# Moving three weight and value requests in a lightning-attention plus feed-forward kernel

## Chip, cores and metric

The kernel runs on one core of one Trainium2 chip. The metric is the time of the device in microseconds (us); less is better. A core has TensorE (matrix products), VectorE, ScalarE and GpSimd (elementwise work), and SyncE (SP), which here only asks for transfers. Transfers (DMAs) are carried by 16 DMA engines that all queues share. In the profile the engines are named PE (its weight loads PEld), DVE, ACT, POOL and SP; a trailing q, as in SPq, is that engine's sequencer, which issues transfers.

## The reference

Two steps. First a block-wise linear attention with decay over 4 batches, 8 heads, 768 positions of 64 elements; then a two-layer feed-forward with the gate h * cos(h).

```python
for b in range(nb):                                   # blocks of 64 positions
    intra = np.einsum('bhic,bhjc->bhij', qb, kb) * Dmask[None]
    intra = np.einsum('bhij,bhjd->bhid', intra, vb)
    inter = np.einsum('bhid,bhde->bhie', qb * lam_pow[None], kv_state)
    out[:, :, sl] = intra + inter
    kv_state = lam_block * kv_state + np.einsum('bhsd,bhse->bhde', kb_dec, vb)
...
x = attn_out as (3072 tokens, 512)
h = x @ w_in            # w_in (512, 2048)
g = h * np.cos(h)
out = g @ w_out         # w_out (2048, 512), result in float32
```

## The kernel before

The 3072 tokens are 24 blocks of 128. The first four blocks are made in two "spans", each of two batches' neighbouring blocks, with a shorter start-up path; the rest come in pairs of blocks (the first pair after the spans, made by `prepare` for blocks 4 and 5, is what the change calls the third pair). The feed-forward runs over tiles of 4, 2, 2, 2, 2, 2, 2, 4 and 4 blocks: for each of 16 column blocks f of w_in, four matmuls make h (L705), ScalarE makes the cosine (L711), VectorE multiplies (L717); then w_out is applied, four f at a time (L749), and the result is copied out (L763) and stored.

For an attention block, q, k and v are loaded in float32. q and v are multiplied by powers of the decay (L341, L349), k is only cast (L345); then q and k are transposed on TensorE (L371), the scores are made (L419) and masked on VectorE (L424), the state is updated (L431, "ps_kv", which needs the scaled v and k), and the values are made (L480, L508). For the third pair ScalarE casts k, GpSimd and VectorE share q and v: the first block's v is scaled by GpSimd and the second block's by VectorE.

The weights are cast on their way in, by DMAs that GpSimd issues: w_in in six pieces (`W_IN = [2, 2, 2, 4, 4, 2]` column blocks of 128) and w_out in four, each piece with four of the 16 rows of blocks. q, k and v of the pairs are asked for by SP (256 KB each), those of the spans by SP (q, k) and by GpSimd (v). Order of the requests is in a string (L35), and `add_w`, `add_load` and `add_span_load` make the requests; their `deps` are transfers that must have landed before this one is issued, set in the loop at L788 to L799: where the kind changes between weights and activations, a request waits for an earlier one of the other kind.

```python
ORDER = "q0 k0 q1 k1 v0 v1 i0 i1 i2 i3 i4 i5 o0 o1 o2 q4 q5 k4 k5 o3"
```

`i2` is the third w_in piece, `o3` the last w_out piece; `v4` and `v5`, the third pair's v, follow from L783 to L785. So `q4` (SP, L266 in the trace) waits for `o1` to land, `o3` for `q4`, and `v4` for `k5`.

The order of instructions on each engine is made by a planner (`Planner.order`) from estimated durations, dependences and priorities, before the kernel is built; engines then run their own lists in order and wait for each other with semaphores. GpSimd's list at the start is: v of both spans, three w_in pieces, two scalings of the second span's k (`k_sp`, L564), three w_in pieces, three w_out pieces, a cast of the state (L679), the last w_out piece, then q and v of the third pair (L341, L349). SP's list after the spans' loads is q4, q5, k4, k5, v4, v5, then q, k and v of the next pair, then stores. The fourth w_in piece also waits for VectorE's first masking of the second span's scores (L588), by a dependence added by hand (L309).

Of the kernel before, what the change touches and what calls it, by code (L numbers as in the profile page):

```python
# [18 lines left out]
SPANS = 2  # L19
# [122 lines left out]
def kernel(  # L142
# [10 lines left out]
    nc = tc.nc  # L153
# [10 lines left out]
    first = [sum(TILES[:i]) for i in range(len(TILES) + 1)]  # L164
# [69 lines left out]
    w_in_sb = consts.tile([P, KD, D_FF], BF16)  # L234
    w_out_sb = consts.tile([P, KF, DM], BF16)
    w_in_src = moe_w_in.rearrange("(ko ki) f -> ki ko f", ki=P)
# [17 lines left out]
    load_t, issue_t = {}, {}  # L254
    last_issue = {}

    def dma(queue, us, issue_us, emit, prio, deps=(), get=None, ordered=True, lat=1.9):
        t = pl.add(queue, issue_us, list(deps) + [last_issue.get(queue) if ordered else None], emit, prio, get=get)
        if ordered:
            last_issue[queue] = t  # L260
        d = pl.add("DMA", us, [t], None, prio, lat=lat)
        d.issue = t
        return t, d

    def start(queue, o, x, deps):
        i = queue.dma_start(out=o, in_=x)  # L266
        for d in deps:
            tc.add_manual_dep(i.ins, d.issue.ins.ins.name, mybir.DependencyInfo(
                mybir.DependencyClass.Sync, mybir.DependencyReason.DATA), reason="order of loads")
        return i  # L270

    def add_span_load(name, src, x, prio, deps):
        def emit(_):
            if on_pool:
                t = span_v[x]
            else:
                if ("raw", x) not in live:
                    live["raw", x] = work.tile([P, 2, H, 2, D], F32, tag="g", name="sp_f")
                t = live[name, "sp", x] = live["raw", x][:, "qk".index(name[0])]
            return start(nc.gpsimd if on_pool else nc.sync, t.rearrange("u h s d -> u h (s d)"),  # L280
                         src[x, :, 0:2 * P, :].rearrange("h (u s) d -> u h (s d)", s=2), deps)

        on_pool = name == "v_f"
        issue, load_t[name, "sp", x] = dma("POOL" if on_pool else "SP", 1.5, 1.0 if on_pool else 0.5, emit, prio, deps,
                                           lat=0.95 if on_pool else 1.0)
        return load_t[name, "sp", x]

    def add_load(n, name, src, prio, deps=()):
        b, c = where(n)

        def emit(_):
            t = loads.tile([P, H, D], F32, tag=name, name=name)
            live[name, n] = t
            return start(nc.sync, t, src[b, :, c * P:(c + 1) * P, :].transpose([1, 0, 2]), deps)

        issue_t[name, n], load_t[name, n] = dma("SP", LOAD_US, 0.85, emit, prio, deps, get=name, lat=1.0)
        return load_t[name, n]

    w_t, w_late = {}, []

    def add_w(which, c, prio, deps=()):
        def emit(_):
            if which == "in":
                a, z = sum(W_IN[:c]) * P, sum(W_IN[:c + 1]) * P
                i = start(nc.gpsimd, w_in_sb[:, :, a:z], w_in_src[:, :, a:z], deps)
                if c == 3:

                    tc.add_manual_dep(i.ins, w_late[0].ins.ins.name, mybir.DependencyInfo(
                        mybir.DependencyClass.Sync, mybir.DependencyReason.DATA), reason="lines of instructions first")  # L309
                return i  # L310
            a, z = c * KF // WCH, (c + 1) * KF // WCH
            return start(nc.gpsimd, w_out_sb[:, a:z, :], w_out_src[:, a:z, :], deps)

        part = W_IN[c] / 4 if which == "in" else 1.0
        early = which == "in" and c < 3
        _, w_t[which, c] = dma("POOL", 2.68 * part, 0.8, emit, -2000.0 if early else prio, deps,
                               lat=1.2)
        return w_t[which, c]
# [231 lines left out]
    def add_span(x):  # L550
# [76 lines left out]
        so, kt, v_t = [[], []], [], [load_t["v_f", "sp", x]]  # L627
        for hp in range(2):
            eq, ek = QK[x]["q"][hp], QK[x]["k"][hp]
            a = pl.add(eq, us[eq], [load_t["q_f", "sp", x]], partial(prep, name="q", hp=hp, e=eq), pa(-0.9 + 0.1 * hp))  # L630
            kt.append(pl.add(ek, us[ek], [load_t["k_f", "sp", x]], partial(prep, name="k", hp=hp, e=ek), pa(-0.9 + 0.1 * hp)))
            if x:
                w_t["in", 3].issue.deps.append(kt[hp])
            outs = []
            for name, src in (("qT", a), ("kT", kt[hp])):
                e = OUTS[x][name][hp]
                t = pl.add("PE", MM(P, 4), [src, s_first if name == "kT" else None], partial(transposes, name=name, hp=hp), pa(-0.5 + 0.1 * hp), banks=1)
                outs.append(pl.add(e, 0.58 if e == "ACT" else 0.42, [t], partial(transposes_out, name=name, hp=hp, e=e), pa(-0.5 + 0.1 * hp)))
                t.bank_frees = [[outs[-1]]]
            s1 = pl.add("PE", 0.42, outs, partial(scores, hp=hp), pa(0.1 + 0.1 * hp), banks=2)  # L640
            if x and hp == 0:

                spans[0]["values"].deps.append(s1)
                s_first = s1
            so[hp] = [pl.add("DVE", 0.69, [s1], partial(scores_out, hp=hp, i=i), pa(0.1 + 0.1 * hp + 0.05 * i)) for i in range(2)]
            s1.bank_frees = [[t] for t in so[hp]]
            if x and hp == 0:
                w_late.append(so[hp][0])

        u = pl.add("PE", 0.42, v_t + kt + [spans[0].get("carried")], update, pv(0.1), banks=1)  # L650
        Uo_sp[x] = [pl.add(e, 0.4 if e == "ACT" else 0.42, [u], partial(update_out, h=h, e=e), pv(0.1))
# [12 lines left out]
    def add_span_state():  # L664


        def update(t):
            live["kv", 1] = bank(t.bank[0], [P, H, D], F32, "ps_kv")
            for h in range(H):
                for s in range(2):  # L670
                    for L, r in zip(spans, halves):
                        nc.tensor.matmul(live["kv", 1][r, h, :], lhsT=L["k"][:, s, h, :], rhs=L["v"][:, s, h, :],
                                         start=(h == 0 and s == 0), stop=True, skip_group_check=True)

        def state(_):
            nc.vector.tensor_copy(new_sum(1, 1), live["kv", 1])  # L676

        def state_16(_):
            nc.gpsimd.tensor_copy(new_S(1, 1), live["sum", 1, 1])  # L679

        u = pl.add("PE", 16 * QUART + SW, span_deps + [w_t["out", 0]], update, LATE, banks=1)
        x = pl.add("DVE", 0.69, [u], state, LATE)
        Uo[1, 1] = pl.add("POOL", 0.61, [x], state_16, LATE)
        u.bank_frees = [[x]]
# [103 lines left out]
    for at, name in enumerate(names):  # L788
        which, n = name[0], int(name[1:])
        soft = which in "io"  # L790
        deps = [kept[-3 if soft else -2]] if at and (names[at - 1][0] in "io") != soft else []
        if name == "o3":
            deps = [load_t["q_f", 2 * SPANS]]
        if soft:
            kept.append(add_w({"i": "in", "o": "out"}[which], n, at, [] if at < 9 else deps))
        elif n < SPANS and at < 9:
            kept.append(add_span_load(which + "_f", src[which], n, at - 2040, kept[0:1] if name == "v0" else []))
        else:
            kept.append(add_load(n, which + "_f", src[which], at, deps))  # L799

    idle = pl.add("SETUP", 0.0, [], None, -1e9, banks=1)
    for x in range(SPANS):
        add_span(x)
    w_t["in", 3].issue.deps += w_late
    add_span_state()
    for pr in range(SPANS, NBLK // 2):
        prepare(pr)
# [69 lines left out]
```

## Time and profile before

| what | value |
|---|---|
| runs | 8, from 205.78 to 207.75 us |
| median | 206.17 us |
| the profiled execution's own time | 205.97 us |
| its span, first to last instruction | 204.3 us |
| TensorE clock granted | 1.000 |
| TensorE busy | 195.3 us |
| VectorE, ScalarE, GpSimd busy | 113.4, 119.2, 64.7 us |
| HBM read, written | 27.27 MB, 6.29 MB |
| first matmul of the feed-forward (L705) | 15.35 us |
| first matmul with w_out (L749) | 30.61 us |
| landing of second and third w_out piece | 29.49, 32.0 us |

Times inside the span are counted from its start. A matmul's row is pipelined: its stated duration overlaps the next one's, so the distance between starts says more than the duration. In lists of waits a row gives the engine, the line that waited, what ended the wait, then total us, times and longest us. In the chain a row gives start, length and what was waited for or worked on.

### The profile page before, as it was taken

The page shows a single profiled execution, that of the slowest core. Times are in us where ns is not written, and L with a number is a line of the kernel's source. Part 1 is how long each engine was busy: PE and PEld are TensorE (multiplying, and loading weights), DVE is VectorE, ACT ScalarE, POOL GpSimd, SP SyncE. Part 2 cuts the span into 40 slices and gives each one's busy share as a digit, 9 for nine tenths or more (in the row PEclk, how much of TensorE's full clock was granted, in tenths as well). Part 3 has the DMA queues.
Part 4 walks back from the last instruction along what each step waited for, and adds up shares of the span by engine and source line. Part 5 has one row for each costly group of instructions (what it writes and reads, how often), then busy time and mean ns, then how long its engine had stood idle before and what let it go on. Part 6 is the DMA issues. An engine that isn't in the chain of part 4 may idle for free.

```text
span 204.3 us, 5936 instructions
## 1 busy us (share of the span) xinstructions
PE 195.3 (96%) x2457; PEld 117.5 (58%) x2485; DVE 113.4 (56%) x221; ACT 119.2 (58%) x232; POOL 64.7 (32%) x85
## 2 busy tenths in 40 slices
PE   6999999999999999999999999999999999999993
PEld 2467444547747848666658766755454444444463
DVE  2887783257953947559557574835687444444001
ACT  5978871128837868466649586745768555354120
POOL 5866004056036263616364244545400000000000
PEclk9999999999999999999999999999999999999999
DMA  4999999989889999999999899999900110111112
GB/s 123 319 190 196 203 202 219 198 196 226 211 205 219 251 219 235 219 196 252 185 262 145 201 226 197 248 153 266 213 0 6 51 51 0 51 55 51 51 71 83
DMA packets 96906, 33.94 MB, mean 166 GB/s; under 512 B 84336, under 2 KB 93936, under 8 KB 96880
## 3 DMA queue, kind: packets, MB, share of 16 engines
q1 hardware_dynamic: 89376, 28.78, 62.3%
q0 software_dynamic: 7360, 4.72, 16.4%
q8 instruction: 19, 0.31, 0.7%
q10 hardware_dynamic: 144, 0.07, 0.1%
q14 instruction: 7, 0.06, 0.1%
HBM read 27.27 MB, written 6.29 MB: 164 GB/s over the span
## 4 chain that ended last, share of the span: by engine, by line
PE 76%; DMA 14%; SPq 3%; POOL 2%; issue 2%; DVE 1%; ACT 0%; POOLq 0%; ACTq 0%
PE ps_f L749 35%; PE ps_h L705 34%; DMA w_out_sb<-in_moe_w_out_dram 6%; DMA v_f<-in_v_dram 3%; DMA sp_f<-in_k_dram 3%; SPq L266 3%; PE ps_o L480 2%; DMA k_f<-in_k_dram 2%; PE ps_kv L431 2%; PE ps_o L508 1%; PE ps_s L419 1%; POOL w_in_sb L266 1%; POOL k_sp L564 1%; DVE v_s L349 0%; POOL w_out_sb L266 0%
## 5 line engine op out<-in xcount | busy, mean ns | idle before, releaser
L717 DVE TENSOR_TENSOR g<-ps_h,cos 128x256 bf16<-128x256 f32 (+1 forms) x148 | 72.9, 503 | 51.4 <-ACT cos L711 50.4
L711 ACT ACTIVATE cos<-ps_h,halfpi 128x256 f32<-128x256 f32 (+1 forms) x148 | 75.8, 539 | 31.4 <-PE ps_h L705 31.0
L705 PE MATMUL ps_h<-xT,w_in_sb 128*128 128x256 bf16 (+1 forms) x587 | 91.3, 304 | 0.3 <-issue 0.2
L749 PE MATMUL ps_f<-w_out_sb,g 128*128 128x512 bf16 (+2 forms) x393 | 88.5, 362 | 2.2 <-issue 1.4
L705 PEld LDWEIGHTS <-w_in_sb 128*128 128x128 bf16 x592 | 57.1, 98 | 30.8 <-DVE xT L516 0.4
L749 PEld LDWEIGHTS <-g 128*128 128x128 bf16 x416 | 38.4, 98 | 35.7
L341 POOL TENSOR_TENSOR qk<-q_f,q_scale 128x512 bf16<-128x512 f32 x19 | 19.7, 1044 | 37.8 <-DMA q_f<-in_q_dram 27.0
L763 ACT COPY o_sb<-ps_f 128x512 f32<-128x512 f32 (+1 forms) x24 | 13.8, 574 | 30.0 <-PE ps_f L749 30.0
L349 POOL TENSOR_TENSOR v_s<-v_f,v_scale 128x512 bf16<-128x512 f32 x19 | 19.5, 1043 | 20.9 <-DMA v_f<-in_v_dram 17.2
L516 ACT CAST xT<-ps_o 128x512 bf16<-128x512 f32 x19 | 10.2, 588 | 11.3 <-PE ps_o L508 8.8
L424 DVE TENSOR_TENSOR s_m<-ps_s,mask 128x512 bf16<-128x512 f32 x20 | 12.9, 683 | 3.3 <-PE ps_s L419 3.0
L345 POOL CAST qk<-k_f 128x512 bf16<-128x512 f32 x18 | 11.0, 614 | 4.6 <-DMA k_f<-in_k_dram 4.5
L437 DVE TENSOR_TENSOR sum<-sum,ps_kv 128x512 f32<-128x512 f32 x15 | 10.2, 682 | 0.8
L442 ACT CAST S<-sum 128x512 bf16<-128x512 f32 x15 | 9.0, 615 | 0.8 <-DVE sum L437 0.7
L480 PEld LDWEIGHTS <-v_s 64*64 64x64 bf16 x320 | 4.3, 106 | 5.0 <-issue 4.4
L763 DVE COPY o_sb<-ps_f 128x256 f32<-128x256 f32 (+1 forms) x2 | 0.7, 358 | 11.2 <-PE ps_f L749 11.2
L480 PE MATMUL ps_o<-s_m,v_s 64*64 64x64 bf16 x320 | 6.4, 198 | 0.5
L837 PE MATMUL ps_idle<-blank 128*128 128x512 f32 (+2 forms) x8 | 5.4, 824 | 1.6 <-DVE blank L209 1.6
L588 DVE TENSOR_TENSOR s_m_sp<-ps_s,mask_sp 128x512 bf16<-128x512 f32 x8 | 5.1, 684 | 1.0 <-PE ps_s L583 1.0
L266 POOL DMA_DIRECT2D w_in_sb<-in_moe_w_in_dram x6 | 4.6, 777 | 1.7 <-DVE s_m_sp L588 1.7
L431 PE MATMUL ps_kv<-v_s,qk 64*64 64x64 bf16 x288 | 4.7, 194 | 0.2 <-DVE v_s L349 0.2
L679 POOL CAST S<-sum 128x512 bf16<-128x512 f32 x1 | 0.6, 607 | 13.0 <-DVE sum L676 13.0
(70 smaller groups left out, 79.3 us busy)
## 6 DMA issues: line engine op xcount, KB each, us to landing
q_f<-in_q_dram SPq DMA_DIRECT2D x20, 256.0 KB, 3.8
k_f<-in_k_dram SPq DMA_DIRECT2D x20, 256.0 KB, 4.6
v_f<-in_v_dram SPq DMA_DIRECT2D x20, 256.0 KB, 5.0
out_dram<-o_sb SPq DMA_DIRECT2D x19, 256.0 KB, 2.4
w_out_sb<-in_moe_w_out_dram POOLq DMA_DIRECT2D x4, 512.0 KB, 11.6
out_dram<-o_sb SPq DMA_DIRECT2D x9, 128.0 KB, 3.3
sp_f<-in_q_dram SPq DMA_DIRECT2D x2, 512.0 KB, 5.2
sp_f<-in_k_dram SPq DMA_DIRECT2D x2, 512.0 KB, 5.6
```

Of the source, the lines that this page charges most:

```text
L266: i = queue.dma_start(out=o, in_=x)
L341: vec[e].tensor_mul(new_qk()[:, 0, :, s], live.pop(("q_f", 2 * pr + s)), q_scale[:, c, :].unsqueeze(2).to_broadcast([P, H, D]))
L345: (nc.scalar.copy if early else nc.gpsimd.tensor_copy)(new_qk()[:, 1, :, s], live.pop(("k_f", 2 * pr + s)))
L349: vec[e].tensor_mul(live["v_s", 2 * pr + s], live.pop(("v_f", 2 * pr + s)), v_scale[:, c, :].unsqueeze(2).to_broadcast([P, H, D]))
L424: nc.vector.tensor_mul(t, live["s", pr][s], mask.unsqueeze(1).to_broadcast([P, H, D]))
L437: nc.vector.tensor_add(new, live["sum", pr, 0] if half else live["sum", pr - 1, 1], live["kv", pr][half])
L480: yield lambda h=h: nc.tensor.matmul(o[halves[h % 2], h // 2, m], lhsT=live["v_s", n0 + s][m, h, :], rhs=live["s_m", n0 + s][m, h, :], sta ...
L705: nc.tensor.matmul(t[:, :n], lhsT=w_in_sb[:, kd, f * P:(f + 1) * P], rhs=live["xT", i][:, kd, at], start=(kd == 0), stop=(kd == KD - 1))
L711: nc.scalar.activation(c[:, :n], live["h", i, f, at.start][:, :n], AF.Sin, bias=halfpi)
L717: nc.vector.tensor_mul(live["g", i][:, f, at], live.pop(("h", i, f, at.start))[:, :n], live.pop(("c", i, f, at.start))[:, :n])
L749: nc.tensor.matmul(live["f", i, j, piece][:, :width], lhsT=live["g", i][:, f, j * P:(j + 1) * P], rhs=w_out_sb[:, f, part], start=(f == 0) ...
L763: (nc.scalar.copy if eng == "ACT" else nc.vector.tensor_copy)(o[:, :width], live["f", i, j, piece][:, :width])
```

## The change

Three requests move. The third w_in piece (`i2`) now waits, in the planner, for the two scalings of the second span's k on GpSimd, so it stands behind them in GpSimd's list; before, the fourth piece had that condition, with one more on VectorE's masking, by plan and by semaphore, and this second one is dropped. The last w_out piece (`o3`) waits for the third to land in place of the third pair's first q. The third pair's first v (`v4`) waits for no landing of k any more. The instructions on all engines stay the same; GpSimd's list differs in the place of one request, and the other engines' lists don't differ.

```diff
-    w_t, w_late = {}, []
+    w_t = {}
 
     def add_w(which, c, prio, deps=()):
         def emit(_):
             if which == "in":
                 a, z = sum(W_IN[:c]) * P, sum(W_IN[:c + 1]) * P
-                i = start(nc.gpsimd, w_in_sb[:, :, a:z], w_in_src[:, :, a:z], deps)
-                if c == 3:
-
-                    tc.add_manual_dep(i.ins, w_late[0].ins.ins.name, mybir.DependencyInfo(
-                        mybir.DependencyClass.Sync, mybir.DependencyReason.DATA), reason="lines of instructions first")
-                return i
+                return start(nc.gpsimd, w_in_sb[:, :, a:z], w_in_src[:, :, a:z], deps)
...
             if x:
-                w_t["in", 3].issue.deps.append(kt[hp])
+                w_t["in", 2].issue.deps.append(kt[hp])
...
-            if x and hp == 0:
-                w_late.append(so[hp][0])
...
         if name == "o3":
-            deps = [load_t["q_f", 2 * SPANS]]
+            deps = [w_t["out", 2]]
+        if name == f"v{2 * SPANS}":
+            deps = []
...
-    w_t["in", 3].issue.deps += w_late
```

## The prediction

> **What bounds the kernel now.** I read the engine table first, then the waits of TensorE, then the chain of waits between 29 and 47 us, and last the order of time on single engines.
>
> ```profile
> PE 195.3 (96%) x2457; PEld 117.5 (58%) x2485; DVE 113.4 (56%) x221; ACT 119.2 (58%) x232; POOL 64.7 (32%) x85
> PE ps_idle L837 <- DVE blank L209: 1.6, 1, 1.6
> PE ps_f L749 <- issue: 1.4, 9, 0.2
> PE ps_t L572 <- POOL k_sp L564: 0.3, 1, 0.3
> PE ps_t L572 <- DVE k_sp L564: 0.3, 1, 0.3
> PE ps_kv L431 <- DVE v_s L349: 0.2, 1, 0.2
> ```
>
> The first row says that TensorE is busy 96% of the span; the others list its waits (engine, line, who ended it: total us, times, longest). Only two of them touch what is changed: 0.3 us for GpSimd's k_sp and 0.2 us for the scaled v. So the change can win little; what it can lose is a new wait.
>
> ```profile
> 16.97 12.52 DMA w_out_sb<-in_moe_w_out_dram
> 31.95 3.77 DMA k_f<-in_k_dram
> 35.73 0.37 SPq L266
> 36.15 6.68 DMA v_f<-in_v_dram
> 42.83 0.02 issue
> 42.85 0.81 DVE v_s L349
> 43.71 0.44 PE ps_kv L431 x30
> ```
>
> This is the chain (start, length, what). Second w_out piece lands at 29.49; the second k lands at 35.72, releases v's request, v lands at 42.83, and VectorE's scaling lets TensorE go on at 43.71. The chain reads as 14% DMA on the page, but TensorE works beside nearly all of it. What matters is where it stands still:
>
> ```profile
> 37.98 0.61 PE L371 MATMUL ps_t<-ident,qk 128*128 128x128 bf16 x8
> 43.31 0.22 PE L431 MATMUL ps_kv<-v_s,qk 64*64 64x64 bf16 x2
> 43.71 0.44 PE L431 MATMUL ps_kv<-v_s,qk 64*64 64x64 bf16 x30 [0.18 <-DVE v_s L349]
> ...
> 35.74 0.62 ACT L345 CAST qk<-k_f 128x512 bf16<-128x512 f32 x1 [0.32 <-DMA k_f<-in_k_dram]
> ...
> 31.48 0.61 POOL L679 CAST S<-sum 128x512 bf16<-128x512 f32 x1 [12.98 <-DVE sum L676]
> 33.46 0.75 POOL L266 DMA_DIRECT2D w_out_sb<-in_moe_w_out_dram  x1 [1.37 <-DMA q_f<-in_q_dram]
> 10.23 2.04 POOL L564 TENSOR_TENSOR k_sp<-sp_f,k_sp 128x512 bf16<-128x512 f32 x2 [0.23 <-DMA sp_f<-in_k_dram]
> 13.97 2.30 POOL L266 DMA_DIRECT2D w_in_sb<-in_moe_w_in_dram  x3 [1.70 <-DVE s_m_sp L588]
> ```
>
> The 32 matmuls of L431 take from 43.31 to 44.15, 0.84 us; the next group of the same kind takes 0.46 us at 56.85. So v's lateness costs 0.38 us in all. The reader should also keep the transposes of k at 37.98: they follow ScalarE's cast, which ends at 36.36.
>
> **What the Trainium skill says.** "DMA: Bandwidth & Descriptors", section "Queues, rings and completion order", says that an engine goes round the queues that have work, and drains one packet, of up to 64 descriptors, before it changes. The trace agrees as to holding out: v was asked for at 35.73, yet in the answer for 36.8 to 38.4 only GpSimd's queue q0 moves packets (the w_out piece asked for at 33.46). No place in it shows a young piece overtaking an older load. The same page, section "Anatomy of one DMA — SWDGE (gpsimd) path", gives a fixed 2.0 us; here the lone w_out piece took 6.4 from issue to landing. "Runtime: NRT & Kernel Launch", section "Instruction fetch mechanics", says that instructions come by DMA in 16 KiB blocks; the page agrees in size (q8: 19 packets, 0.31 MB).
>
> **The change part by part.** The profiled execution took 205.97 us (span 204.3, 1.67 around it); sums are made against it. The median of the runs, 206.17, lies 0.20 above. No instruction is added or removed on any engine: TensorE, VectorE, ScalarE and SP keep their order, GpSimd moves one instruction, and waits change.
>
> *Third w_in piece.* GpSimd's third issue (0.78 us, 9.21 to 9.99) goes behind its two scalings of k. They then have GpSimd from 9.21, but need k, which lands at 10.06 (4.07 + 5.99 in the chain), so they start at some 10.15 instead of 10.23, and end near 12.2 (VectorE's k_sp starts 0.09 after its landing of 6.99). Bounds: gain 0 to 0.1; I take 0.05, off the 0.33 wait of TensorE at 11.33.
> The piece itself is issued at about 12.25 instead of 9.21. Before, it needed 8.9 us to land (18.1). Its first user is the fifth column block, after 20 more matmuls of 0.109 from 16.91: 19.09. In the queue ahead stand v and two pieces, and the engines are full (0.85 MB of q0 alone in the answer for 10.0 to 14.5), so a later request mostly waits less: the next piece, of double size, took 6.2, and 12.25 + 6.2 = 18.5. Cost 0, hidden by the 28 matmuls of the first two pieces; if landing took 8.9 again, 12.25 + 8.9 - 19.09 = 2.1 us.
>
> *The fourth w_in piece without its wait for VectorE.* The 1.70 us idle of GpSimd before 13.97 goes. Pieces four to six and three of w_out follow at 12.25 + 0.77 = 13.0 instead of 13.97, all moved up by 0.95 in the one queue. They land one after the other at the engines' rate (29.49 and 32.0 for the last two: 2.5 us each), so landings move by 0 to 0.3; TensorE waits for none of them now. Gain 0. The removed wait is labelled as keeping lines of instructions ahead of the piece. Without it a block of TensorE's instructions may queue behind one piece more (2.5 us); TensorE's rows show no wait of that kind, so I take 0.
>
> *The third pair's v.* SP asks for it after k's issue ends (31.95 + 0.82 = 32.8), not at 35.73: 2.9 us sooner. SP's next requests (two q, two k, two v of the fourth pair, from 36.78) move up with it, and one of those took 4.13 to issue; nothing of TensorE waits for them. The scaling on VectorE can start when its two masks are done, 40.81 + 1.29 = 42.10, and must start by 43.31 - 0.80 = 42.5. So v has to come only 0.4 us sooner than 42.83 for the whole 0.38 to go. Bounds: gain 0 to 0.38; I take 0.38.
>
> *The last w_out piece.* It now waits for the third piece (17.70 + 14.3 = 32.0) instead of a q that landed at 32.9, and stands behind the cast that ends at 32.09. Between wait and issue lay 0.54 before, so it starts at 32.15 to 32.55, about 1.1 us sooner. Behind it on GpSimd stands the scaling of q (34.22), which then starts with q's landing at 33.8, 0.3 sooner; TensorE's transposes of q at 35.80 were not waiting. First use of the piece is at 42.36 and it landed at 39.86: no gain. Its traffic now meets the second k's. That is the rival below; I take 0.
>
> Sum: -0.05 - 0 - 0.38 - 0 = -0.43 us, that is 205.5 for the execution and about 205.75 for a median; rounded, 205.8. Late next is nothing: TensorE's other waits are 0.1 to 0.16 us each, at its own changes of shape.
>
> **The rivals.**
> A, the forecast: 205.8.
> B, slower: the last w_out piece overtakes k. Before, it was issued at 33.46, and narrow windows of the DMA answer show q0's first packets at 34.9, 1.44 later; now that is 33.6 to 34.0. The two k landed at 34.78 and 35.72, so the second was moving from about 34.0. If the piece comes first on even one engine, that k is later by one piece, 2.55, up to 3.55 with the near empty microsecond that the answer for 35 to 36 shows at its start. Slack: 37.98 - 0.62 - 0.05 - 35.72 = 1.57. Loss 1.0 to 2.0, net of 0.43: 0.55 to 1.55, middle 207.2. It decides from a k landing after 37.3. For it: v stood behind this piece before. Against it: k is asked for at 31.95, 0.2 to 0.6 us earlier, by the faster path.
> C, nothing: the piece goes before v as now, and one late engine keeps v's landing at 42.8; the wait for v stays. 206.1. Against it: the idle microsecond at 35 to 36 is filled, which is more than 0.4.
> D, the third w_in piece lands after 19.1, or instructions come late: +0.5 to +2.1, 207.3.
> E, a gain that I don't see, from other loads coming sooner: 205.0. Against it: TensorE's remaining waits don't hang on loads.
>
> **How the numbers follow.** A 0.53, B 0.25, C 0.13, D 0.05, E 0.04. A measurement can tell about 0.5%, 1.03 us, from no change. Slower by that: half of B, all but a little of D, 0.03 for what I overlook: 0.20. Faster: E and the far edge of A: 0.05. Same: 0.75. The range goes from A less 0.5 (both waits of 0.33 and 0.38 gone, and noise) to the upper part of B: 205.3 to 207.3.
>
> **What would show it.** Right: k_sp starts at 10.1 to 10.2; the third w_in issue stands at 12.25 and lands before 19; v is issued near 32.8 and the group of L431 runs its 32 matmuls in 0.46; the cast of the second k stays near 35.7. B shows as an idle TensorE before the transposes at 37.98 with ScalarE's cast named; D as a wait of L705 near 19 us. I am wrong if a wait of over 0.2 appears on TensorE that is not among these.

## The result and the profile after

The changed kernel takes 208.63 us in the median (11 runs, 207.36 to 212.48) against 206.30 (32 runs of the kernel before beside it, 205.60 to 207.75): a ratio of 1.0106 [1.0081, 1.0131], slower. All ratios here leave out runs over 1.5% above the fastest of the same kernel as disturbed, among them three of the changed kernel (210.92, 211.19, 212.48), though these turn out below to be part of the effect.

The profiled execution took 210.14 us, with a span of 208.4; before, 205.97 and 204.3. So 4.1 us are to be found. All line numbers of the changed kernel are lower: L366 is L371 of before (transposes), L340 is L345 (cast of k), L426 is L431 (state), L742 is L749 (w_out), L414 is L419 (scores).

From the page of the kernel after, the engine table and the granted TensorE clock in 40 slices of 5.2 us:

```profile
PE 197.1 (95%) x2457; PEld 118.3 (57%) x2485; DVE 113.6 (54%) x221; ACT 119.3 (57%) x232; POOL 64.8 (31%) x85
...
PEclk9999999969999999999999999999999999999999
```

TensorE has the same 2457 matmuls, but is busy 1.8 us longer, and one slice of its clock, at 41.7 to 46.9 us, is at 0.6. So there are two losses: a wait, and matmuls at a lower clock. The waits of the kernel after (engine, line, what ended the wait: total us, times, longest) show the first:

```profile
PE ps_t L366 <- ACT qk L340: 2.5, 1, 2.5
...
PE ps_f L742 <- issue: 1.6, 9, 0.3
```

A wait of 2.5 us stands before one group of transposes; it did not exist before. The row of TensorE for the scaled v is gone. The chain of the kernel after (start, length, what) leads from that wait back to its cause:

```profile
31.98 8.06 DMA k_f<-in_k_dram
40.04 0.02 issue
40.06 0.63 ACT qk L340
40.69 0.05 issue
40.73 0.62 PE ps_t L366 x8
```

The second k of the third pair is on its way for 8.06 us; before it was 3.77. It lands at 40.04 instead of 35.72, ScalarE casts it, and only then can TensorE go on. In order of time, TensorE and then GpSimd (start, duration, idle time before in brackets):

```profile
36.31 1.89 PE L742 MATMUL ps_f<-w_out_sb,g 128*128 128x512 bf16 x8
40.73 0.62 PE L366 MATMUL ps_t<-ident,qk 128*128 128x128 bf16 x8 [2.54 <-ACT qk L340]
41.19 2.94 PE L742 MATMUL ps_f<-w_out_sb,g 128*128 128x512 bf16 x8
...
47.63 0.45 PE L426 MATMUL ps_kv<-v_s,qk 64*64 64x64 bf16 x32
...
10.29 2.04 POOL L559 TENSOR_TENSOR k_sp<-sp_f,k_sp 128x512 bf16<-128x512 f32 x2 [0.97 <-DMA sp_f<-in_k_dram]
12.28 3.04 POOL L266 DMA_DIRECT2D w_in_sb<-in_moe_w_in_dram  x4
...
32.33 0.75 POOL L266 DMA_DIRECT2D w_out_sb<-in_moe_w_out_dram  x1 [0.18 <-issue]
```

The reader is to see four things. Eight w_out matmuls take 1.89 us before the standstill, and eight of the same shape take 2.94 after it. The state's 32 matmuls now take 0.45 without a break (0.84 before). The four w_in pieces leave GpSimd at 12.28 as one row. And the last w_out piece leaves at 32.33, 1.13 us sooner than before (33.46), 0.35 after k's transfer began at 31.98.

By windows of the kernel after (busy us of TensorE, its loads, VectorE, ScalarE and GpSimd, granted clock, DMA share, GB/s):

```profile
40.70:42.00 1.30, 1.27 (x12) 0.86 (x13) 0.61 (x1) 0.00 (x0) 0.94 (x1) 0.95 1.04 237
42.00:44.00 2.00, 2.00 (x5) 0.45 (x3) 0.08 (x1) 0.00 (x0) 1.15 (x2) 0.50 1.09 248
44.00:46.00 2.00, 1.67 (x37) 1.08 (x38) 1.18 (x2) 0.00 (x0) 1.75 (x3) 0.68 1.15 261
```

TensorE runs at half clock from about 41.9 to 45.3. The lost time is length times one less clock: 1.3 x 0.05 + 2.0 x 0.50 + 2.0 x 0.32 = 1.7 us. The transposes themselves start 2.75 us later than before (40.73 against 37.98); the wait counts 2.54 of it, as rows overlap. The sum is 2.75 (wait) + 1.7 (clock) - 0.38 (v's wait gone) = 4.07 of the 4.1 us. The starts of rows give the clock's part as 1.57: from the transposes to the state's matmuls it is 6.90 us, and it was 5.33. By these starts the kernel is 3.94 us behind at that place; the last 0.2 of the 4.1 come near 117 us, away from the change.

Not every execution has the second loss. Of the 12 of the changed kernel, six have a mean clock of 0.998 or more and take 207.36 to 208.63 us; six have 0.992 or less and take 209.48 to 212.48. The first six have a middle of 208.4, which is 2.1 above before, near the wait less v's gain (2.75 - 0.38 = 2.37 in the execution shown). Of 137 executions of the kernel before that stood beside the later runs, one fell below 0.997 (0.992, 209.45 us).

Why was k late? Of the transfers between 36.0 and 38.4 us of the kernel after, by queue (packets, MB, share of the 16 engines), and then the only queue of that window in the kernel before:

```profile
q0 software_dynamic: 374, 0.37, 96.5%
q1 hardware_dynamic: 362, 0.09, 23.1%
...
q0 software_dynamic: 395, 0.40, 108.9%
```

q0 is GpSimd's queue, with the w_out piece; q1 is SP's, with k and, behind it, v. Before, k was complete by then and q0 was alone. Now most of the engines' time goes to the piece while k is unfinished. The semaphore records of the trace show it by parts: a load gives 16 signals of landing, as many as there are engines, and the last of them is what the waiting engine is released by. Before, all 16 of k came between 35.16 and 35.72. Now eight came from 35.28 to 36.04, a ninth at 37.09, and the other seven only from 38.96 to 40.04, while the piece's own came from 38.11 to 39.87. It reads as seven parts of k that stood still until the piece was through on their engines, though the records don't name the engine of a signal. The piece itself landed at 39.87, where it had landed at 39.86 before.

### The profile page after: what moved, and what is told of

Read it like the earlier page. It is cut to its first block, busy times and chain, and to the rows that moved or that the text cites. A ratio compares the mean times of both kernels' runs of the same rounds, so it can differ in the third digit from the quotient of the medians.

```text
span 208.4 us, 5935 instructions
## 1 busy us (share of the span) xinstructions
PE 197.1 (95%) x2457; PEld 118.3 (57%) x2485; DVE 113.6 (54%) x221; ACT 119.3 (57%) x232; POOL 64.8 (31%) x85
## 4 chain that ended last, share of the span: by engine, by line
PE 77%; DMA 13%; POOL 3%; SPq 3%; issue 2%; ACT 0%; POOLq 0%; ACTq 0%
PE ps_f L742 37%; PE ps_h L698 34%; DMA w_out_sb<-in_moe_w_out_dram 6%; DMA k_f<-in_k_dram 4%; DMA sp_f<-in_k_dram 3%; SPq L266 2%; PE ps_o L475 2%; PE ps_s L414 2%; PE ps_kv L426 1%; POOL w_in_sb L266 1%; PE ps_o L503 1%; POOL k_sp L559 1%; POOL w_out_sb L266 0%; ACT qk L340 0%; PE ps_t L366 0%
## 5 line engine op out<-in xcount | busy, mean ns | idle before, releaser
L742 PE MATMUL ps_f<-w_out_sb,g 128*128 128x512 bf16 (+2 forms) x393 | 89.6, 365 | 2.3 <-issue 1.6
L742 PEld LDWEIGHTS <-g 128*128 128x128 bf16 x416 | 38.7, 98 | 36.4 <-issue 1.3
L419 DVE TENSOR_TENSOR s_m<-ps_s,mask 128x512 bf16<-128x512 f32 x20 | 12.9, 683 | 4.5 <-PE ps_s L414 4.3
L340 POOL CAST qk<-k_f 128x512 bf16<-128x512 f32 x18 | 11.0, 614 | 5.7 <-DMA k_f<-in_k_dram 5.6
L340 ACT CAST qk<-k_f 128x512 bf16<-128x512 f32 x2 | 1.2, 617 | 8.6 <-DMA k_f<-in_k_dram 8.6
L369 DVE COPY qkT<-ps_t 128x1024 bf16<-128x1024 bf16 x2 | 1.4, 690 | 7.0 <-PE ps_t L366 7.0
```

The costliest lines, as they stand in the source:

```text
L340: (nc.scalar.copy if early else nc.gpsimd.tensor_copy)(new_qk()[:, 1, :, s], live.pop(("k_f", 2 * pr + s)))
L419: nc.vector.tensor_mul(t, live["s", pr][s], mask.unsqueeze(1).to_broadcast([P, H, D]))
L742: nc.tensor.matmul(live["f", i, j, piece][:, :width], lhsT=live["g", i][:, f, j * P:(j + 1) * P], rhs=w_out_sb[:, f, part], start=(f == 0) ...
```

## The experiments

Four theories stood at the start. O: the last w_out piece, asked for sooner, takes k's turn. V: v, asked for sooner, does it. W: the w_in edit does it, by moving the whole stream. C: the standstill costs clock as well, beyond its own length. Later runs ask how the turns go. The runs of the kernel before beside them had medians of 206.42 (first four), 206.43 (the next four) and 206.55 us (the last two).

**The change without the last w_out piece's edit.**

```diff
         if name == "o3":
-            deps = [w_t["out", 2]]
+            deps = [load_t["q_f", 2 * SPANS]]
```

> The changed kernel with the last w_out piece waiting for the third pair's first q again; the other two edits stay. Theory O (the last w_out piece, asked for sooner, gets in front of the second k on some of the engines): the second k lands near 35.7 us again, TensorE's 2.5 us wait at the transposes of k is gone, and the time is that of before less the 0.4 us of my sum: 205.6 to 206.2, ratio 0.997 to 1.000. Theory V (v's requests, 2.9 us sooner, crowd the second k): the k still lands after 37.3 and the ratio stays at or above 1.006. Theory W (the third w_in piece behind GpSimd's scaling) also leaves the ratio at or above 1.006.

Measured: 205.93 us (20 runs), ratio 0.9979 [0.9965, 0.9994]. The order of time on TensorE:

```profile
37.98 0.61 PE L366 MATMUL ps_t<-ident,qk 128*128 128x128 bf16 x8
...
43.32 0.45 PE L426 MATMUL ps_kv<-v_s,qk 64*64 64x64 bf16 x32
```

The piece is issued at 33.48 again, k lands at 36.07, and the transposes stand at 37.98 as before. The edits of w_in and v are all there, so neither V nor W makes the loss, nor do both together. What is left of the change is a gain of 0.2%. It is not a shift of all runs: the fastest takes 205.57 us, where the kernel before has 205.53, but none of the 20 is above 207, where 8 of 41 of the kernel before are.

**The last w_out piece's edit alone, in the kernel before.**

```diff
         if name == "o3":
-            deps = [load_t["q_f", 2 * SPANS]]
+            deps = [w_t["out", 2]]
```

> The kernel before with only the last w_out piece waiting for the third piece. Theory O: the second k lands at 39 to 40.5, TensorE waits 2 to 3 us before the transposes of k, ratio 1.008 to 1.016; v still waits for that k, so v lands some 6 us later than before and a second wait at L431 of up to 2 us can follow. Theory V or W: no change of over 0.3 us, ratio 0.998 to 1.002.

Measured: 210.82 us (6 runs, 207.96 to 212.91), ratio 1.0147 [1.0094, 1.0200]. TensorE in order of time:

```profile
43.40 1.03 PE L371 MATMUL ps_t<-ident,qk 128*128 128x128 bf16 x8 [5.21 <-ACT qk L345]
```

Issued at 32.46, the piece landed at 40.95 and k at 42.70, so TensorE stood 5.2 us in this execution, the slowest of the six. Here all 16 signals of k came after 38.8; 15 of them were in by 40.67, and one was 2 us later. The edit alone makes the loss; that it makes a larger one than the whole change is not shown, as the intervals overlap and the two runs at full clock took 207.96 and 208.54. The second wait at L431 did not come: these 32 matmuls run in 0.54 us without a break from 50.59. The clock was at one half for 6.8 us, and the transposes run at it (1.03 us for 0.61). A row of the windows shows that it was so before TensorE went on:

```profile
40.40:43.40 3.00, 0.01 (x1) 0.01 (x1) 0.00 (x0) 0.62 (x1) 0.00 (x0) 0.50 0.05 9
```

**The change, with the piece issued behind GpSimd's scaling of the second q.**

```diff
+        qk_head["last", pr] = a[1]
...
+    o3 = w_t["out", 3].issue
+    plan.remove(o3)
+    plan.insert(plan.index(qk_head["last", SPANS]) + 1, o3)
```

> The changed kernel with one instruction moved on GpSimd: the request for the last w_out piece stands behind the scaling of the third pair's second q, so that it is issued near 35.0 instead of 32.3; its wait stays as changed. Theory O: that is behind the start of the second k's transfer, k lands at 35.7, v before 40, the piece at 41 to 42, just ahead of its first use at 42.36: ratio 0.996 to 0.999; should the piece land after 42.4, TensorE waits for it there. Theory V: as the changed kernel, ratio at or above 1.006.

Measured: 206.83 us (22 runs), ratio 1.0006 [0.9988, 1.0024]. The piece leaves at 34.74 and k lands at 35.44, so k is safe. But both v now go before the piece (36.77 and 38.97), and it lands at 43.02 after 8.3 us. TensorE in order of time:

```profile
43.06 1.02 PE L743 MATMUL ps_f<-w_out_sb,g 128*128 128x512 bf16 x4 [0.47 <-DMA w_out_sb<-in_moe_w_out_dram]
```

Its first user stood ready 0.47 us sooner, and no gain was measured where 0.1 to 0.4% had been expected. So the piece has a window: early, it delays k, and late, v delays it.

**The change, with 48 more transposes of q before those of k**, into the same bank, where TensorE would stand idle; they are overwritten.

```diff
+            if i and pr == SPANS:
+                for _ in range(6):
+                    for h in range(H):
+                        nc.tensor.transpose(live["t", pr, i][:, h, :], live["qk", pr][:, 0, h], ident)
```

> The changed kernel with 48 more transposes of q (8 made six times over, written to the same bank that the transposes of k then overwrite) in front of the transposes of k, so that TensorE works during most of the wait. Theory C (the drop of the granted clock to 0.5 for 3.4 us that follows the wait comes from TensorE standing still): k still lands near 40, but the granted clock stays 1.00 and no run is above 209.5; median 208.2 to 208.9. Theory N (the drop has to do with something else): the clock drops as often as in the changed kernel, where it was below 0.995 in 6 of 12 runs.

Measured: 208.62 us (6 runs, 208.37 to 209.54), ratio 1.0112 [1.0086, 1.0139]. TensorE in order of time, and then a row of the windows:

```profile
38.07 2.84 PE L368 MATMUL ps_t<-ident,qk 128*128 128x128 bf16 x48
```

```profile
42.00:44.00 2.00, 2.00 (x41) 0.94 (x39) 0.50 (x2) 0.00 (x0) 1.18 (x2) 1.00 0.84 190
```

The fill takes as long as the standstill did, so the median is no better; but the clock in the window that had 0.50 is 1.00, and all six runs have a mean clock of 0.997 or more. In the changed kernel six of 12 lost it; were that one half here too, six runs without a loss would be one chance in 64. So TensorE lost its clock because it stood still.

**v's edit alone, in the kernel before.**

```diff
+        if name == f"v{2 * SPANS}":
+            deps = []
```

> The kernel before with only the wait of v for the second k taken away. My sum: the 32 matmuls of L431 run in 0.46 us instead of 0.84, so -0.38 us, ratio 0.998, between 0.9965 and 0.9995, with the second k landing within 0.5 of 35.7. A theory by which v's early requests alone hold up k: k after 37.3 and ratio above 1.003.

Measured: 206.38 us (22 runs), ratio 0.9993 [0.9972, 1.0013]. TensorE in order of time, and then an issue in the DMA answer for the second v (KB, us to landing):

```profile
43.75 0.44 PE L431 MATMUL ps_kv<-v_s,qk 64*64 64x64 bf16 x30 [0.25 <-DVE v_s L349]
```

```profile
v_f<-in_v_dram SPq DMA_DIRECT2D x1, 256.0 KB, 9.1
```

v is asked for at 32.81 and 33.84, 2 to 3 us sooner, and lands at 40.85 and 42.98. The second v used to land at 42.83. The wait for it stays: an earlier request does not bring it forward. Ten of the first v's 16 signals came by 37.64, ahead of the w_out piece's (39.31 to 42.05, where it had landed at 39.86), but all those of the second v came after 40.1. Two of the 22 runs took 209.49 and 209.57 us at a clock of 0.992 or less. v may have delayed k in those, but no profile of them exists, and one run of 137 of the kernel before was like them.

**The w_in edit alone, in the kernel before**: the third piece behind the scaling of k, the fourth without its waits.

```diff
-                if c == 3:
+                if False:
...
-                w_t["in", 3].issue.deps.append(kt[hp])
+                w_t["in", 2].issue.deps.append(kt[hp])
...
-    w_t["in", 3].issue.deps += w_late
```

> The kernel before with only the third w_in piece behind GpSimd's scaling and the hand-made wait of the fourth piece gone. My sum: -0.05 us, ratio 0.998 to 1.002; the third piece lands near 18, before its first use at 19.1, and TensorE shows no wait at L705 over 0.1. A theory by which this edit carries part of the loss: a wait at L705 or at an instruction's start, ratio above 1.003. A theory by which it carries the 0.2% that the two edits together win: ratio near 0.998.

Measured: 205.76 us (22 runs), ratio 0.9978 [0.9961, 0.9995]. TensorE in order of time:

```profile
43.33 0.45 PE L431 MATMUL ps_kv<-v_s,qk 64*64 64x64 bf16 x32
```

The wait for the scaled v is gone here, with v's own dependence in place. The second w_out piece lands at 29.34 (29.49 before), the requests that hang on it come a little sooner, and v lands at 41.51 and 42.41, just under the 42.5 that was worked out in the prediction. That the 0.15 us did this is argued: the last of 16 parts decides, and in the kernel before 15 parts of the second v were in by 41.15 and one came at 42.83. As in the run without the last piece's edit, the fastest runs are no faster (205.52 against 205.50) and the slow ones are rarer: 1 of 22 above 207, where 15 of 59 were. The estimates say that the w_in edit gives as much as w_in and v together and v's nothing; the intervals of the two single edits overlap, so it is not shown that v's share is nothing.

**The change, with a GpSimd copy of 128 x 512 float32 ahead of the piece's issue**, to put it half way.

```diff
+            if c == 3:
+                nc.gpsimd.tensor_copy(pad, blank)
```

> The changed kernel with one copy of 128x512 float32 on GpSimd (some 0.6 us, its result unused) ahead of the last w_out piece's issue, which then comes near 32.9, between 32.3 (k lands at 40) and 33.5 (k lands at 36.1). Theory O says that it depends on which of the two reaches an engine first: at 32.9 the piece should pass k on fewer engines or on none; k lands at 36 to 40, and the wait of TensorE is between 0 and 2.5 us. A theory of shared bandwidth, in which k is only slowed in proportion to the overlap, gives k near 38 and a wait near 0.7.

Measured: 206.94 us (20 runs), ratio 1.0010 [0.9982, 1.0038]. In the profiled execution the piece leaves at 32.61, k lands at 36.46 and TensorE does not wait for it. But the runs fall into groups: ten at 205.6 to 206.4, six at 207.5 to 207.9, and four at 208.6 to 209.6, two of these at a clock of 0.992. The same instructions in the same order give good and bad times with the piece 0.28 us later than in the changed kernel. That k's landing makes the groups is argued, as only one execution was profiled; runs of the kernel before reach 208.40 at full clock too, so the middle group may have another cause.

**Eight ScalarE copies before the cast of the second k, in the kernel before**: a standstill of TensorE that no transfer makes. (The requests from the third pair's q on come 0.4 to 0.8 us later than before; k landed at 36.50 and waited for ScalarE.)

```diff
+            if pr == SPANS and s:
+                for _ in range(8):
+                    nc.scalar.copy(pad, blank)
```

> The kernel before, with its own transfers, and eight copies of 128x512 float32 on ScalarE (results unused) in front of the cast of the third pair's second k, so that TensorE stands still some 2.3 to 3 us before the transposes of k, with no transfer moved. Theory C (standing still costs the clock): the granted clock falls below 0.995 in about half of the runs, as in the changed kernel, and the time is up by the wait, 2.3 to 3 us, or by 4 to 5 us where the clock falls. Theory N: clock at 1.00 in all runs, time up by the wait alone.

Measured: 211.44 us (6 runs, 209.47 to 211.58), ratio 1.0217 [1.0177, 1.0257]. TensorE in order of time, and then a row of the windows:

```profile
41.88 0.62 PE L375 MATMUL ps_t<-ident,qk 128*128 128x128 bf16 x8 [3.52 <-ACT qk L349]
```

```profile
43.00:45.00 2.00, 2.00 (x6) 0.57 (x4) 0.23 (x1) 0.00 (x0) 1.28 (x2) 0.50 1.03 233
```

Five of six runs have a clock of 0.992 or less and take some 5 us more than before; the sixth, at 0.999, takes 209.47, which is 3.0 more. The standstill is longer than the 2.3 to 3 us expected. One of 3.5 us costs itself and, mostly, nearly 2 us of clock.

**The same with five copies.**

```diff
-                for _ in range(8):
+                for _ in range(5):
```

> As the run with eight copies on ScalarE, but with five: TensorE stands still some 1.6 to 1.9 us before the transposes of k, no transfer moved. Theory C with a threshold: at under 2 us the granted clock stays above 0.995 in all runs or nearly all, and the time is up by the wait alone, 1.6 to 1.9 us (ratio 1.006 to 1.010). Theory C without one: the clock falls in about half of the runs here too.

Measured: 207.52 us (18 runs, 206.89 to 208.25), ratio 1.0042 [1.0023, 1.0060]. TensorE in order of time:

```profile
39.75 0.62 PE L375 MATMUL ps_t<-ident,qk 128*128 128x128 bf16 x8 [1.41 <-ACT qk L349]
```

All 18 runs keep a clock of 0.997 or more. A standstill of 1.4 us costs about 1 us and no clock; 1.6 to 1.9 had been expected of both.

**The change, with the last w_out piece as two requests of half the size, one right after the other.**

```diff
+            if c == 3:
+                start(nc.gpsimd, w_out_sb[:, a:a + 2, :], w_out_src[:, a:a + 2, :], deps)
+                a += 2
```

> The changed kernel with the last w_out piece asked for as two DMAs of half the size, one right after the other. Theory O with turns (an engine that has work in two queues finishes one DMA's share of one queue, then takes the other queue): k is passed by the first half alone, lands 1.3 to 1.9 us later than its 35.7, near 37.3, so TensorE waits 0 to 0.6 us: ratio 0.998 to 1.004. Theory O with first come, first served: k waits for both halves wherever it waits at all and the time is that of the changed kernel, ratio 1.007 to 1.014.

Measured: 207.12 us (20 runs, 206.41 to 211.62), ratio 1.0032 [1.0009, 1.0055]. TensorE in order of time:

```profile
38.91 0.62 PE L369 MATMUL ps_t<-ident,qk 128*128 128x128 bf16 x8 [0.78 <-ACT qk L343]
```

The halves leave at 32.23 and 32.92 and land at 38.19 and 39.85; k lands at 38.22, between them. The same bytes, asked for as early as in the changed kernel, now delay k by 2.50 instead of 4.32 us, more than the 1.3 to 1.9 that were expected. Were the two queues served in the order of asking, cutting the piece would change nothing. Were the engines shared evenly between them, all parts of k in the changed kernel would be late; but eight come within 0.32 us of the last of before, and seven over 3 us after it. So it is turns: an engine takes a piece of one queue's work, then of the other's, and a smaller piece is a shorter turn. An estimate of a turn: 374 packets of the piece took 96.5% of 16 engines for 2.4 us, 0.1 us each; 0.37 MB in 374 packets makes some 512 of them for the 512 KB, 32 for each engine, 3.2 us. Between the early and the late signals of k lie 2.9 us (36.04 to 38.96). So a turn was about an engine's whole share of the piece, as far as one profile shows. Four of the 20 runs still took 209.49 us or more at a clock of 0.992 or less.

## Why the prediction was wrong

The forecast was 205.8, and 208.63 lies above its range too. The mechanism was on its list, as rival B with a chance of 0.25.

- *The step that failed: "The last w_out piece", where the meeting of its traffic with the second k's was taken at 0.* It moved the transposes by 2.75 us. Taking the edit away removes the loss (0.9979), and the edit alone makes it (1.0147). The argument used against B, that k is asked for 0.2 to 0.6 us earlier and by the faster path, is what the runs overturn. k's transfer did begin 0.35 before the piece's issue, and the piece's first packets came even later than B had it, at 34.5 (33.6 to 34.0 was said), 2.2 after the issue. But k was unfinished then, since the first k had to be moved before it and landed only at 35.04; and being first does not hold an engine. "DMA: Bandwidth & Descriptors", section "Queues, rings and completion order", says that an engine goes round the queues that have work. The prediction quoted this and used it only for a young load behind an old piece. It is true the other way round, as the run with two halves supports.
- *B's size.* One piece was priced at 2.55 to 3.55 us; k was 4.32 later. The slack was right: 4.32 - 1.57 = 2.75, which is what the transposes moved (its sum as written gives 1.59; the 0.02 are the issue after the landing). Less the 0.38, B came to +2.1 in executions at full clock, not to +0.55 to +1.55.
- *The clock was in no step.* In half of the executions a further 1.7 us goes there. Filling the standstill keeps the clock (none of six runs loses it), and a standstill that ScalarE makes loses it (5 of 6).
- *The third w_in piece: right as to its cost.* GpSimd starts scaling k at 10.29 (10.15 was said, 10.23 before), so the 0.05 us of gain did not come; the piece leaves at 12.28 (12.25) and lands at 17.95 (at most 18.5). TensorE does not wait at 19.09.
- *The fourth w_in piece: right at its own place, wrong in what it brings.* No wait for instructions appears. "Gain 0" was wrong for the two w_in edits together (0.9978 alone): in that profile the second w_out piece lands 0.15 us sooner and v under 42.5. Which of the two does it was not tried.
- *The third pair's v: right as to the request (32.85 for 32.8) and the 0.38, wrong as to the cause.* No gain of v's edit alone is measured (0.9993, interval 0.9972 to 1.0013), and in its profile the wait is still there. Rival C, that the piece goes before v and v lands late, holds there for the second v, which TensorE waits for.
- *What would show it.* The sign named for B, an idle TensorE before the transposes with ScalarE's cast named, is just what the page shows.

The best version of those that ran leaves the last w_out piece where it was: 0.9979 [0.9965, 0.9994] with v's edit and 0.9978 [0.9961, 0.9995] without. Open are why seven parts of k were passed in the changed kernel's profile and all 16 with the edit alone, how large a turn is beyond the one estimate, and how long TensorE may stand in one stretch of the clock (below) between 1.41 and 2.19 us. A piece sent early and held by a semaphore until k has landed was not tried.

## What to carry to other kernels

Before a transfer is asked for sooner, list what is still moving on the other queues when its first packets come, and who waits for it: engines go in turns, the older request is not safe, and the last of 16 engines decides the landing. Price the loss as at least a whole turn of the new transfer, cut a large transfer where a small urgent one runs beside it, and add the clock if TensorE would stand for over about 2 us. An edit whose gain is a wait that goes away should be run alone, since here another edit of the same change took that wait away without it.

## What the hardware showed that was not expected

- A standstill cost TensorE its clock in 6 of 12 executions of the changed kernel (2.54 us in the one profiled) and in 5 of 6 with eight copies (3.52 us); with five copies (1.41 us) it was 0 of 18. "TensorE: Matmul & The Clock Gate", section "Part 1: The HAM clock gate", gives a free-running activity window of 3.4 us. The traces agree: a slow spell lasts 3.41 us in two profiles and 6.83 in the third, and each begins a whole number of 3.413 us after the trace's first record of full clock (10 in the changed kernel, 11 with eight copies, 10 with the last piece's edit alone). Its rule against idle gaps of over some 3.4 us (under "HAM oscillation — how this bites in real kernels") is too mild here: 2.5 us was enough in half of the executions.
- What counts is the standstill inside one such stretch. The stretch before each fall of the clock held 2.27 us of it (changed kernel), 2.30 (eight copies) and 2.19 (the last piece's edit alone); with five copies all 1.41 us lay in one stretch and the clock stayed. So the limit lies between 1.41 and 2.19 in these traces. With the last piece's edit alone the clock fell at 40.38, 3 us before TensorE went on, so going on is not what starts the spell. An estimate from these figures, if the limit is 2.1 and the stretches begin at random: 2.54 us lose the clock in 0.51 of the executions and 3.52 us in 0.80, against 6 of 12 and 5 of 6.
- One kernel, with one order of instructions and the piece issued half way, has times from 205.61 to 209.55 us, with none between 206.4 and 207.5. Its one profile showed no wait for k at all.
